# A forgetting attention and a gated convolution FFN on one core: the order of all 1,056 pieces of work written anew

## The chip, the core and the metric

The kernel runs on one core of a Trainium2 chip. The time is the device time of one launch in microseconds (us): the median of three runs was 245.37 us before the change (244.91 to 245.58). Everything said of the inside of a run comes from one profiled execution of the kernel before.

## What is computed

For each of 8 batches: an attention over 8 heads (576 tokens, 64 wide) whose scores carry a decay, then a feed-forward layer whose gate is a convolution of width 3 along the tokens.

```python
# attention, per batch and head: q, k, v [576, 64], f [576]
scores = q @ k.T / 8
cum    = cumsum(log(clip(f, 1e-4, 1)))
scores = where(j > i, -1e9, scores + cum[i] - cum[j])
attn   = softmax(scores) @ v                       # -> x [576, 512] over 8 heads
# feed-forward, per batch
h    = maximum(x @ w_in, 0)                        # [576, 1024]
conv = sum_k conv_w[k] * shift(h, k - 1)           # along the tokens
out  = (h * sigmoid(conv)) @ w_out                 # [576, 512], float32
```

## The kernel before

The work is cut into small named pieces, and a string `ORDER` lists them all in the order in which they are written into the program. Each engine (TensorE is PE in the profile, VectorE DVE, ScalarE ACT, GpSimd POOL, SyncE SP with its DMA queue) gets its own pieces in that order and works through them in order, so `ORDER` fixes what stands behind what on every engine and on every DMA queue. A piece that may run on several engines carries the engine behind an `@`. `ORDER` also decides which buffer a piece gets: there are four PSUM buffers (`ps0` to `ps3` in the rows below), and a piece that needs one takes the buffer that was given back longest ago in the list.

```python
for x in order:
    name, _, engine = x.partition("@")
    ...
    for r in t["take"]:
        self.slot[name, r] = free[r].pop(0)
```

The pieces, by the letters in `ORDER` (the head group `hb`, 0 to 15, is half of a batch, four heads; `i` is a pair of heads, 0 to 31; `b` is a batch; `ff` is one of eight slices of 128 hidden channels):

- Loading q and k. For `hb` 0 and 1: `ld` (DMA), nine transposes on TensorE (`tp`, L166), copied out of PSUM by ScalarE or VectorE (`cl`, L172 or L174). From `hb` 2 on: a transposing DMA (`q`, L180), for `hb` 2 to 7 followed by a clean-up on VectorE (`cl`, L186) and by two small DMAs of decay rows (`rw`, L204 and L205) from a table in HBM (`image`). That table is made once: the chain `dca`, `dcl` (the logarithm, L268 on ScalarE, then a table load), `dcs`, `dck` ends in the tile `kc`, and `ki` stores it with three DMAs (L281).
- v: DMAs `v`, casts to fp16 `va` (L219, and L221 for the last 64 tokens).
- Weights: DMAs `wi`, `wo` (L518), casts `wic`, `woc` (L526).
- Scores on TensorE: `sd` (diagonal blocks), `so` (the rest), `st` (the last 64 tokens), all L314. Their exponentials on ScalarE: `ed` (L355), `eo` (L372), `et` (L334). From `hb` 8 on the causal mask is laid on by GpSimd selects `md` and `mt` (L358, L337).
- `pv` on TensorE (attention times v, L391 and L396), `n` and `m` on VectorE (divide by the row sums, L405 and L407), `t` on TensorE and `tx` on VectorE or ScalarE (turn the result, L416 and L419; a DMA for `hb` 11 to 15).
- Feed-forward of batch `b`: `f` (L431) on TensorE, `r` (relu, L442) on ScalarE, `c` and `d` (the convolution: two VectorE operations that read two tensors each, L448 and L450), `a` (the gate's curve, L453) on ScalarE, `g` (gate times h, L460 or L458) on VectorE, `o` (L476) on TensorE, `e` (copy out, L481, L492) on ScalarE or VectorE, `s` (store).

The first feed-forward product `f0.0` needs both head groups of batch 0 turned (`tx0`, `tx1`), and `f1.0` those of batch 1 (`tx2`, `tx3`). After every `f` come `r`, `c`, `d`, `a`, `g` on two engines, and all eight `g` of a batch before its `o`. The list is a mix of the attention of later head groups and the feed-forward of earlier batches.

## Time and profile before

| what | value |
|---|---|
| median of the runs shown | 245.37 us (244.91 to 245.58) |
| the profiled execution: its span, first to last instruction | 244.7 us |
| TensorE busy | 228.6 us (93%) |
| ScalarE busy | 206.8 us (85%) |
| VectorE busy | 205.5 us (84%) |
| GpSimd busy | 51.9 us (21%) |
| first product of the feed-forward (`f0.0`) | at 37.30 us |
| first product of batch 1's feed-forward (`f1.0`) | at 63.23 us |
| last matmul ends | at 240.7 us |

The profiled execution has no device time of its own beside its span; the median of the runs lies 0.67 us above the span, and that part is taken as it is. Times inside the run are counted from the first instruction. "Busy" joins overlapping instructions of an engine; an engine that shows two instructions with x2 started the second before the first had ended.

### The profile page before, as it was taken

The page shows a single profiled execution, that of the slowest core. Times are in us where ns is not written, and L with a number is a line of the kernel's source. Part 1 is how long each engine was busy: PE and PEld are TensorE (multiplying, and loading weights), DVE is VectorE, ACT ScalarE, POOL GpSimd, SP SyncE. Part 2 cuts the span into 40 slices and gives each one's busy share as a digit, 9 for nine tenths or more (in the row PEclk, how much of TensorE's full clock was granted, in tenths as well). Part 3 has the DMA queues.
Part 4 walks back from the last instruction along what each step waited for, and adds up shares of the span by engine and source line. Part 5 has one row for each costly group of instructions (what it writes and reads, how often), then busy time and mean ns, then how long its engine had stood idle before and what let it go on. Part 6 is the DMA issues. An engine that isn't in the chain of part 4 may idle for free.

```text
span 244.7 us, 6393 instructions
## 1 busy us (share of the span) xinstructions
PE 228.6 (93%) x2627; PEld 146.1 (60%) x2627; DVE 205.5 (84%) x324; ACT 206.8 (85%) x278; POOL 51.9 (21%) x77
## 2 busy tenths in 40 slices
PE   0899889879999999999999999999999999999993
...
GB/s 189 334 169 250 278 184 189 223 198 306 196 216 196 169 182 220 238 268 251 224 212 274 194 198 269 270 102 196 265 198 227 195 209 4 106 173 77 171 85 216
DMA packets 120424, 49.68 MB, mean 203 GB/s; under 512 B 109879, under 2 KB 110647, under 8 KB 120395
## 3 DMA queue, kind: packets, MB, share of 16 engines
...
q10 hardware_dynamic: 322, 0.47, 0.6%
...
HBM read 21.11 MB, written 10.17 MB: 128 GB/s over the span
## 4 chain that ended last, share of the span: by engine, by line
PE 81%; DMA 5%; DVE 5%; ACT 5%; issue 1%; SPq 1%; ACTq 0%; DVEq 0%
PE ps L476 26%; PE ps L431 23%; PE ps L314 15%; PE ps L391 7%; DMA qk<-image 3%; PE ps L322 3%; PE ps L396 3%; DMA u<-in_f_dram 2%; PE ps L416 2%; ACT qk L172 2%; DVE u L450 2%; DVE u L448 1%; ACT ht L442 1%; ACT pp L372 1%; PE ps L317 1%
## 5 line engine op out<-in xcount | busy, mean ns | idle before, releaser
L431 PE MATMUL ps<-xt,w_in_f 128*128 128x512 f16 (+1 forms) x512 | 71.0, 288 | 0.4 <-DVE xt L419 0.4
L372 ACT ACTIVATE pp<-ps 128x1024 f16<-128x1024 f32 x64 | 64.8, 1032 | 3.7 <-PE ps L314 2.3
L476 PE MATMUL ps<-w_out_f,hg 128*128 128x512 f16 x288 | 66.8, 379 | 0.0
L314 PE MATMUL ps<-qk 128*128 128x128 bf16 (+2 forms) x576 | 63.9, 241 | 2.1 <-DMA qk<-image 0.9
L448 DVE SCALAR_TENSOR_TENSOR u<-ht,cwt 128x576 f32<-128x576 f16 x64 | 52.4, 832 | 4.4 <-ACT ht L442 4.2
L450 DVE SCALAR_TENSOR_TENSOR u<-ht,cwt,u 128x576 f32<-128x576 f16 x64 | 53.9, 856 | 0.5
L453 ACT ACTIVATE hg<-u,cw 128x576 f16<-128x576 f32 x64 | 48.7, 782 | 6.1 <-DVE u L450 6.0
L431 PEld LDWEIGHTS <-w_in_f 128*128 128x128 f16 x512 | 34.7, 99 | 29.4 <-issue 1.3
L314 PEld LDWEIGHTS <-qk 128*128 128x128 bf16 x576 | 39.4, 98 | 19.2 <-issue 2.5
L442 ACT ACTIVATE ht<-ps 128x576 f16<-128x576 f32 x64 | 41.0, 664 | 6.4 <-PE ps L431 2.8
L476 PEld LDWEIGHTS <-hg 128*128 128x128 f16 x288 | 26.9, 98 | 28.9
L460 DVE SCALAR_TENSOR_TENSOR hg<-hg,ht 128x576 f16<-128x576 f16 x51 | 38.6, 767 | 0.6 <-ACT hg L453 0.5
L358 POOL TENSOR_SCALAR_AFFINE_SELECT pp<-pd 128x1024 f16<-128x1024 f32 x16 | 19.7, 1244 | 53.6 <-ACT pd L355 53.6
L391 PE MATMUL ps<-va,pp 128*128 128x65 f16 x640 | 25.3, 194 | 1.7 <-DVE va L219 1.7
L391 PEld LDWEIGHTS <-pp 128*128 128x128 f16 x640 | 23.0, 98 | 4.2 <-DVE va L219 1.9
L407 DVE TENSOR_TENSOR xm<-ps,rc 128x896 f16<-128x896 f32 (+1 forms) x32 | 23.9, 751 | 0.5
L355 ACT ACTIVATE pp<-ps 128x1024 f16<-128x1024 f32 x16 | 16.6, 1038 | 5.2 <-PE ps L314 4.0
L219 POOL CAST va<-vf 128x1024 f16<-128x1024 f32 x8 | 10.0, 1247 | 34.3 <-PE ps L314 18.8
L355 ACT ACTIVATE pd<-ps 128x1024 f32<-128x1024 f32 x16 | 16.2, 1023 | 1.2 <-PE ps L314 0.5
L405 DVE RECIPROCAL rc<-ps 128x14 f32<-128x14 f32 (+1 forms) x32 | 6.6, 207 | 10.2 <-PE ps L396 4.9
L322 PE MATMUL ps<-mask,ident 128*128 128x512 bf16 (+1 forms) x40 | 14.4, 364 | 0.4 <-ACT pp L372 0.3
L481 ACT COPY ob<-ps 128x1024 f32<-128x1024 f32 (+1 forms) x14 | 12.9, 918 | 0.3 <-issue 0.2
...
## 6 DMA issues: line engine op xcount, KB each, us to landing
...
```

What stands on the lines that cost most here:

```text
L314: nc.tensor.matmul(o, tk[:, h * S + k0:h * S + k0 + 128], tq[:, h * S + q0:h * S + q0 + n], start=first, stop=last and not by_matmul(hb, h))
L355: nc.scalar.activation(o, ps_of(f"sd{i}").rearrange("p (s c) -> p s c", s=2), AF.Exp, scale=SCALE)
L372: nc.scalar.activation(pair(i)[:, s, 512:1536], ps_of(f"so{i}.{s}"), AF.Exp, scale=SCALE)
L391: nc.tensor.matmul(ps[:, c:c + D + 1], block(hb, h, m, n), va[:, h, m, 0:D + 1], start=(m == 0), stop=(m == n))
L407: nc.vector.tensor_tensor(xm[:, CUT * D * u:CUT * D * u + nj * k * D].rearrange("p (j x d) -> p j x d", x=k, d=D), got[:, :, :, 0:D], r.un ...
L431: nc.tensor.matmul(ps[:, t0:t1], w_in_f16[:, cc, 128 * ff:128 * (ff + 1)], xt[:, cc // 2, x:x + t1 - t0], start=(cc == 0), stop=(cc == NCC ...
L442: nc.scalar.activation(ht_of(b, ff)[:, 2:2 + S], ps_of(f"f{b}.{ff}")[:, 0:S], AF.Relu, scale=1.0 if (b, ff) in LATE else 0.5)
L448: nc.vector.scalar_tensor_tensor(u, ht[:, 1:1 + S], cwt[:, ff, 0:1], ht[:, 2:2 + S], op0=ALU.mult, op1=ALU.add)
L450: nc.vector.scalar_tensor_tensor(u, ht[:, 3:3 + S], cwt[:, ff, 1:2], u, op0=ALU.mult, op1=ALU.add)
L453: nc.scalar.activation(hg_of(b, ff), u_t[slot[f"c{b}.{ff}", "u"]], AF.Sigmoid if (b, ff) in LATE else AF.Tanh, scale=cw[:, ff, 1:2])
L460: nc.vector.scalar_tensor_tensor(hv, hv, 1.0, ht_of(b, ff)[:, 2:2 + S], op0=ALU.add, op1=ALU.mult)
L476: nc.tensor.matmul(ps[:, 512 * j:512 * (j + 1)], w, w_out_f16[:, ff, :], start=(ff == 0), stop=(ff == NFF - 1))
```

## The change

`ORDER` is replaced as a whole; no function and no instruction's shape is touched. The same 1,056 pieces stand in another order, and 38 of them name another engine:

- From GpSimd to VectorE: `va0.0`, `va0.1`, `va1.0`, `va6.0`, `va14.1`, `wic1`, `woc0`, `woc2`, `woc3`. From GpSimd to ScalarE: `va5.0`, `va9.1`, `va10.0`. To GpSimd: `va3.1`, `va7.1`, `va8.0`, `va12.1` from ScalarE, `va4.1`, `va7.0`, `va8.1`, `va9.0` from VectorE. GpSimd keeps its selects.
- From VectorE to ScalarE: `va1.1`, `cl1.1.0`, `tx0`, `e4.0`, `e7.3`, `e7.0`. From ScalarE to VectorE: `cl1.1.1`, `tx2`, `tx10`, `va11.1`, `e2.1`, `e7.1.0`, `e7.2`, `e7.4`.
- DMAs: `ki`, `rw1` and `s7.4` go from SyncE's queue to ScalarE's, `rw5` from ScalarE's to SyncE's.

The first two lines of the new list and of the old one:

```diff
-dca cw ld0 ld1 ld0.0.0 tp0.0.0 dcl ld0.1.0 ld0.0.1 tp0.0.1 tp0.1.0 v0.0 ld0.1.1 ld1.0.1 ld1.0.0 dcs dck v0.1 v0.2 ...
+ld0 ld0.0.0 dca tp0.0.0 ld0.0.1 tp0.0.1 cl0.0.0@ACT ld1 ld0.1.1 cl0.0.1@ACT v0.0 ld1.0.0 dcl cw ld0.1.0 tp1.0.0
+cl1.0.0@ACT v0.4 tp0.1.0 tp0.1.1 ld1.0.1 dcs cl0.1.0@ACT dck q2.0 cwt ki@ACT sd0 tp1.0.1 q2.1 tp1.1.0 cl0.1.1@DVE
```

The new `ORDER` has more lines, so a line of the changed kernel is 51 higher than the same line before (L172 is L223 there).

ScalarE at the start of the program. The row on `u0` is the logarithm `dcl`; rows with `qk` from `ps` are the copies `cl` of the turned q and k (`qk0` belongs to `hb` 0, `qk1` to `hb` 1); rows with `pp` are exponentials. Before:

```order
L268 ACTIVATE u0_120<-u0_120 128x576 [waits DMAHW2_49,DMAHW0_49,DVE_49]
L269 ACT_TABLE_LOAD
L172 ACTIVATE qk0_85<-ps1_130,lim_76 128x1152 [waits PE_49]
L172 ACTIVATE qk0_85<-ps2_131,lim_76 128x1152 [waits PE_49]
L172 ACTIVATE qk0_85<-ps3_132,lim_76 128x1152 [waits PE_49]
L355 ACTIVATE pp0_95<-ps2_131 128x2x512 [waits PE_49]
```

After:

```order
L223 ACTIVATE qk0_85<-ps0_129,lim_76 128x1152 [waits DVE_49,PE_49]
L223 ACTIVATE qk0_85<-ps1_130,lim_76 128x1152 [waits DVE_49,PE_49]
L319 ACTIVATE u0_120<-u0_120 128x576 [waits DMAHW2_49,DMAHW0_49,DVE_49]
L320 ACT_TABLE_LOAD
L223 ACTIVATE qk1_86<-ps3_132,lim_76 128x1152 [waits PE_49]
L223 ACTIVATE qk0_85<-ps0_129,lim_76 128x1152 [waits PE_49]
L332 DMA image_65<-kc_73 64x576 [waits DMAHW7_49,DVE_49]
L332 DMA image_65<-kc_73 64x576 [waits DMAHW0_49]
L332 DMA image_65<-kc_73 64x576 [waits DMAHW2_49,DVE_49]
L406 ACTIVATE pp0_95<-ps3_132 128x2x512 [waits PE_49]
```

Two copies now stand ahead of the logarithm, a copy for `hb` 1 (out of `ps3`, which the first exponential's scores take next) ahead of the third, and the three stores of the decay table stand in ScalarE's queue.

VectorE from the first value casts to the second turned tile, without the head of the list (`xt0` is batch 0's turned attention: the last row before is `tx1`, with `tx0` three rows above it). Before:

```order
L186 TENSOR_SCALAR qk2_87<-qk2_87,lim_76 128x2304 [waits DMAHW1_49]
L405 RECIPROCAL rc0_110<-ps1_130 128x14 [waits PE_49,Activation_49]
L407 TENSOR_TENSOR xm0_108<-ps1_130,rc0_110 128x896 [waits DVE_49]
L405 RECIPROCAL rc1_111<-ps1_130 128x4 [waits PE_49]
L407 TENSOR_TENSOR xm0_108<-ps1_130,rc1_111 128x256 [waits DVE_49]
L405 RECIPROCAL rc2_112<-ps3_132 128x14 [waits PE_49,Activation_49]
L407 TENSOR_TENSOR xm1_109<-ps3_132,rc2_112 128x896 [waits DVE_49]
L419 COPY xt0_113<-ps1_130 128x1152 [waits PE_49]
L405 RECIPROCAL rc0_110<-ps0_129 128x4 [waits PE_49,Activation_49]
L407 TENSOR_TENSOR xm1_109<-ps0_129,rc0_110 128x256 [waits DVE_49]
L419 COPY xt0_113<-ps3_132 128x1152 [waits PE_49]
```

After:

```order
L270 CAST va0_91<-vf0_89 128x4x4x64 [waits DMAHW6_49,DMAHW5_49,DMAHW1_49]
L270 CAST va1_92<-vf0_89 128x4x4x64
L272 CAST va1_92<-vf0_89 64x4x64
L237 TENSOR_SCALAR qk2_87<-qk2_87,lim_76 128x2304 [waits DMAHW4_49]
L456 RECIPROCAL rc0_110<-ps0_129 128x14 [waits PE_49,Activation_49]
L458 TENSOR_TENSOR xm0_108<-ps0_129,rc0_110 128x896 [waits DVE_49]
L577 CAST w_in_f16_69<-ob0_125 128x2x512 [waits DMAHW3_49]
L456 RECIPROCAL rc1_111<-ps2_131 128x4 [waits PE_49,Activation_49]
L458 TENSOR_TENSOR xm0_108<-ps2_131,rc1_111 128x256 [waits DVE_49]
```

(then `n1`, `m1` of `hb` 1 and one copy, `tx1`). Three value casts and a weight cast came in, and the copy `tx0` went to ScalarE.

VectorE around `tx3`, the copy into `xt1` that lets `f1.0` start (`u` rows are `c` and `d`, `hg` rows are `g`). Before:

```order
L186 TENSOR_SCALAR qk1_86<-qk1_86,lim_76 128x2304
L419 COPY xt1_114<-ps3_132 128x1152
L450 SCALAR_TENSOR_TENSOR u2_122<-ht4_119,cwt_72,u2_122 128x576
L460 SCALAR_TENSOR_TENSOR hg_124<-hg_124,ht3_118 128x576
L460 SCALAR_TENSOR_TENSOR hg_124<-hg_124,ht2_117 128x576
L460 SCALAR_TENSOR_TENSOR hg_124<-hg_124,ht0_115 128x576
L460 SCALAR_TENSOR_TENSOR hg_124<-hg_124,ht1_116 128x576
L460 SCALAR_TENSOR_TENSOR hg_124<-hg_124,ht4_119 128x576
L448 SCALAR_TENSOR_TENSOR u1_121<-ht3_118,cwt_72 128x576
```

After:

```order
L470 COPY xt1_114<-ps1_130 128x1152
L237 TENSOR_SCALAR qk1_86<-qk1_86,lim_76 128x2304
L499 SCALAR_TENSOR_TENSOR u2_122<-ht4_119,cwt_72 128x576
L511 SCALAR_TENSOR_TENSOR hg_124<-hg_124,ht3_118 128x576
L501 SCALAR_TENSOR_TENSOR u2_122<-ht4_119,cwt_72,u2_122 128x576
L511 SCALAR_TENSOR_TENSOR hg_124<-hg_124,ht0_115 128x576
L511 SCALAR_TENSOR_TENSOR hg_124<-hg_124,ht2_117 128x576
L511 SCALAR_TENSOR_TENSOR hg_124<-hg_124,ht1_116 128x576
L511 SCALAR_TENSOR_TENSOR hg_124<-hg_124,ht4_119 128x576
L577 CAST w_out_f16_70<-ob1_126 128x1024
L577 CAST w_out_f16_70<-ob0_125 128x1024
L499 SCALAR_TENSOR_TENSOR u3_123<-ht3_118,cwt_72 128x576
```

The clean-up `cl5.1` and the convolution half `c0.7` moved from ahead of the copy to behind it, and weight casts (`woc3`, `woc0`, a few rows later `woc2`) now stand on VectorE.

More of the change, by code (lines that the diff above doesn't have):

```diff
@@ new lines @@
+ld0 ld0.0.0 dca tp0.0.0 ld0.0.1 tp0.0.1 cl0.0.0@ACT ld1 ld0.1.1 cl0.0.1@ACT v0.0 ld1.0.0 dcl cw ld0.1.0 tp1.0.0
+cl1.0.0@ACT v0.4 tp0.1.0 tp0.1.1 ld1.0.1 dcs cl0.1.0@ACT dck q2.0 cwt ki@ACT sd0 tp1.0.1 q2.1 tp1.1.0 cl0.1.1@DVE
+cl1.0.1@DVE sd1 v0.3 tp1.1.1 ed0 v0.2 cl1.1.0@ACT ed1 so1.1 v0.1 so0.1 so1.0 wi1 cl1.1.1@DVE cl2.0 va1.0@DVE st0 wi0
+rw1@ACT eo0.1 wic0@POOL va0.0@DVE so0.0 eo1.0 eo1.1 wi2 sd2 wic2@POOL va0.1@DVE cl2.1 rw2@SP et0 eo0.0 so2.1 ed2 pv0.0
+eo2.1 so2.0 sd3 n0.0 m0.0 so3.0 eo2.0 q3.0 st1 wic1@DVE q3.1 ed3 pv0.1 et1 so3.1 eo3.0 eo3.1 sd5 va1.1@ACT ed5 pv1.0
@@ new lines @@
+pv1.1 n0.1 m0.1 t0 n1.0 m1.0 n1.1 m1.1 so5.1 tx0@ACT t1 sd4 eo5.1 ed4 wi3 tx1@DVE f0.0 cl3.1 q4.1 r0.0 so4.1 cl3.0
+f0.1 f0.2 eo4.1 r0.1 v1.0 v1.3 c0.0 so4.0 d0.0 f0.3 wic3@POOL rw3@SP so5.0 r0.2 eo4.0 h0 q4.0 f0.4 c0.1 v1.2 r0.3 v1.1
+eo5.0 f0.5 a0.0 r0.4 wo3 c0.2 st2 et2 v1.4 d0.2 cl4.1 d0.1 g0.0 a0.2 st3 sd6 c0.3 r0.5 c0.4 ed6 so6.1 g0.2 eo6.1 d0.4
+d0.3 q5.0 sd7 va2.0@DVE f0.6 so7.1 ed7 eo7.1 va3.0@ACT c0.5 va3.1@POOL pv2.0 et3 q5.1 va2.1@POOL cl4.0 so6.0 n2.0 d0.5
+r0.6 a0.4 m2.0 rw4@ACT g0.4 wo1 so7.0 f0.7 c0.6 pv2.1 n2.1 eo6.0 eo7.0 r0.7 d0.6 pv3.0 pv3.1 a0.5 m2.1 v2.0 sd9 cl5.0
@@ new lines @@
+t2 n3.0 n3.1 v2.1 a0.3 m3.0 v2.2 a0.1 m3.1 ed9 so9.1 a0.6 tx2@DVE t3 st4 et4 sd8 tx3@DVE eo9.1 f1.0 cl5.1 woc1@POOL
+ed8 so9.0 eo9.0 c0.7 g0.3 r1.0 wo0 d0.7 so8.1 g0.5 g0.6 f1.1 eo8.1 f1.2 f1.3 a0.7 f1.4 r1.2 v2.4 rw5@SP g0.1 g0.7 r1.1
+v2.3 r1.3 woc3@DVE sd10 r1.4 wo2 woc0@DVE q6.0 ed10 c1.0 c1.2 so10.1 st5 et5 sd11 q6.1 woc2@DVE c1.1 c1.3 d1.2 q7.0
+d1.3 q7.1 so11.1 f1.5 eo10.1 o0.0 va5.0@ACT ed11 d1.1 d1.0 o0.1 o0.2 va4.0@ACT eo11.1 va5.1@ACT h1 v3.0 f1.6 cl6.0
+a1.2 c1.4 cl6.1 a1.1 e0.0@ACT rw6@SP g1.1 va4.1@POOL g1.2 a1.3 v3.2 v3.1 so10.0 a1.0 o0.3 r1.5 so8.0 r1.6 f1.7 cl7.0
@@ new lines @@
+eo10.0 v3.3 eo8.0 e0.1@ACT g1.3 c1.5 so11.0 pv4.0 d1.4 d1.5 pv4.1 cl7.1 eo11.0 r1.7 n4.0 m4.0 zc pv5.0 n4.1 a1.4 n5.0
+sd13 m4.1 pv5.1 m5.0 so13.1 a1.5 va7.0@POOL n5.1 ed13 sd12 rw7@SP c1.7 m5.1 c1.6 eo13.1 t4 so13.0 t5 ed12 tx4@DVE
+so12.0 eo13.0 sd15 tx5@DVE g1.4 eo12.0 va6.0@DVE q9.1 f2.0 d1.7 ed15 so12.1 g1.0 r2.0 eo12.1 f2.1 d1.6 st7 q9.0 a1.7
+c2.0 et7 so15.1 pv6.0 g1.7 a1.6 r2.1 f2.2 v4.0 v3.4 f2.3 eo15.1 q8.1 n6.0 st6 m6.0 sd14 g1.6 c2.1 r2.3 d2.0 et6 g1.5
+r2.2 ed14 so15.0 c2.2 h2 q8.0 c2.3 f2.4 d2.2 so14.1 f2.5 eo15.0 a2.0 r2.5 o1.0 a2.2 so14.0 eo14.1 d2.3 g2.0 va7.1@POOL
@@ new lines @@
+fi9 r2.4 c2.5 o1.1 d2.5 eo14.0 a2.5 e1.0@ACT c2.4 f2.6 fi8 g2.2 pv7.0 va6.1@POOL sd18 pv7.1 d2.1 v4.4 r2.6 n7.0 pv6.1
+m7.0 ed18 n7.1 g2.5 a2.1 n6.1 m7.1 m6.1 sd16 ed16 so16.0 eo16.0 g2.1 v4.2 t7 t6 tx6@DVE f2.7 v5.0 v4.1 tx7@DVE sd19
+f3.0 o1.2 a2.3 d2.4 r2.7 q10.1 st9 md18 c2.7 r3.0 md16 ed19 v4.3 c2.6 d2.6 q11.0 so18.0 a2.4 va8.0@POOL c3.0 a2.6 g2.6
+et9 eo18.0 g2.3 md19 va8.1@POOL s1.0 sd17 ed17 q11.1 o1.3 q10.0 f3.1 so19.1 so19.0 md17 d2.7 g2.4 d3.0 e1.1@ACT r3.1
+f3.2 f3.3 mt9 eo19.1 va9.0@POOL so17.0 eo19.0 s0.0 o1.4 a2.7 eo17.0 h3 r3.2 r3.3 a3.0 g2.7 fi11 f3.4 c3.1 d3.1 so18.1
```

28 lines of the change are left out of this document (27 added, 1 removed).

## The prediction

> **What bounds the kernel now.** I read the page first: the busy shares, the slices and the chain of waits.
>
> ```profile
> span 244.7 us, 6393 instructions
> PE 228.6 (93%) x2627; PEld 146.1 (60%) x2627; DVE 205.5 (84%) x324; ACT 206.8 (85%) x278; POOL 51.9 (21%) x77
> PE   0899889879999999999999999999999999999993
> PE 81%; DMA 5%; DVE 5%; ACT 5%; issue 1%; SPq 1%; ACTq 0%; DVEq 0%
> ```
>
> TensorE is most of the chain, and its slices have holes in the first quarter only. Next, the busy time by stretch (length, then PE, PEld, DVE, ACT, POOL busy, granted clock, DMA share, GB/s):
>
> ```profile
> 10.00:20.00 10.00, 9.92 (x120) 8.29 (x119) 5.19 (x12) 7.74 (x8) 1.37 (x2) 1.00 1.01 221
> 20.00:30.00 10.00, 9.23 (x122) 6.89 (x120) 4.48 (x5) 7.89 (x10) 3.06 (x3) 1.00 1.05 270
> 37.30:63.20 25.90, 22.75 (x293) 15.14 (x290) 24.30 (x36) 22.55 (x33) 4.59 (x4) 0.93 1.10 226
> 63.20:88.10 24.90, 24.90 (x288) 15.32 (x286) 23.32 (x33) 23.62 (x33) 3.17 (x2) 1.00 0.98 197
> 88.10:240.70 152.60, 152.56 (x1659) 92.24 (x1659) 139.37 (x211) 136.06 (x189) 32.27 (x33) 1.00 0.86 193
> ...
> 38.20:63.10 24.90, 22.00 (x283) 14.71 (x283) 23.51 (x36) 21.73 (x32) 4.59 (x4) 0.93 1.09 234
> 63.10:86.70 23.60, 23.60 (x255) 14.25 (x254) 22.02 (x32) 22.63 (x32) 3.17 (x2) 1.00 0.98 194
> ```
>
> From 63 us to 240.7 TensorE has no gap (24.90 of 24.90, 152.56 of 152.60). So the end of the program is the moment at which TensorE reaches a given piece, plus the matmuls that are left. The pieces ahead of `f0.0`, between `f0.0` and `f1.0`, and between `f1.0` and `sd12` (where 88.08 stands below) are the same sets in both lists, only shuffled; so the time of `sd12` decides, if TensorE stays without gaps behind it. Between `f0.0` and `f1.0` TensorE works 22.75 of 25.90 us, part of it at half clock (mean 0.93, worth 1.8 us): about 20.9 us of matmul at full clock in 25.9. Who holds it up there? The waits of TensorE between 37 and 63 us (who waits, for whom: total, times, longest):
>
> ```profile
> PE ps L391 <- DVE va L219: 1.7, 1, 1.7
> PE ps L314 <- DVE xm L407: 0.5, 1, 0.5
> PE ps L431 <- DVE xt L419: 0.4, 1, 0.4
> PE ps L416 <- DVE xm L407: 0.3, 1, 0.3
> ```
>
> VectorE, four times in a row, and it is busy 23.51 of 24.90 us there. It is the bound from 38 to 63 us, and close to it up to 87 (22.02 of 23.60).
>
> **The change, part by part.** The rows for the prices (start, busy, engine, line; in brackets the idle time ahead and its releaser), first the head of the program:
>
> ```profile
> 9.65 3.71 ACT L172 ACTIVATE qk<-ps,lim 128x1152 uint16<-128x1152 uint16 x3
> 10.26 0.76 DVE L276 SCALAR_TENSOR_TENSOR kc<-u,kc 64x576 bf16<-64x576 f32 x1
> 12.22 0.58 PE L322 MATMUL ps<-mask,ident 128*128 128x512 bf16 x1
> 23.25 1.43 SPq L518 DMA_DIRECT2D ob<-in_moe_w_in_dram  x3
> 25.15 7.33 DMA qk<-image
> 32.52 0.40 PE L314 MATMUL ps<-qk 128*128 128x128 bf16 x4 [0.86 <-DMA qk<-image]
> 35.75 0.75 DVE L419 COPY xt<-ps 128x1152 f16<-128x1152 f16 x1
> 37.51 0.76 DVE L419 COPY xt<-ps 128x1152 f16<-128x1152 f16 x1 [0.46 <-PE ps L416]
> ```
>
> 1. *The head, up to `tx1`* (ends 37.51 + 0.76 = 38.27). Two copies (3.71 / 3 = 1.24 each) now run ahead of the logarithm, which takes nothing from it; but the first scores `sd0` take the buffer that the copy `cl1.0.0` empties behind the logarithm. They start at 12.22 now. Ends: 1.2 earlier (`kc` is ready at 10.26 + 0.76 = 11.02, and nothing else is in the way), or one copy, 1.2, later. I take 1.0 later, since that copy waits for the fifth load of the queue and stands behind the table load. ScalarE, which must empty every score buffer, idles 2.26 and 2.11 us of the two slices from 10 to 30; it gives one copy to VectorE and takes one, so this delay is made up by about 25 us. The gain comes behind it. Now the decay rows of `hb` 2 are issued behind three weight loads (23.25 x3) and land 7.33 us later, and `sd5` waits for them until 32.52. In the new list the weight loads stand directly behind the value loads, several microseconds ahead of the rows, and `sd5` is reached at about 30.4 without that wait. What follows is ScalarE's exponentials, so only some 1.3 of these 2.1 us reach `pv1.0`. The copy `tx0` (0.75, of which 0.67 to the next start) leaves VectorE, where `n1.1`, `m1.1` and `tx1` stood behind it. The four casts that VectorE gets there (0.6 each) lie in its idle time: it works 4.48 of 10 us from 20 to 30. Sum: -1.3 - 0.67 = -2.0, `tx1` ends at 36.3. Ends: -3 (all of `sd5`'s 2.1 counts) and +1 (the delay of `sd0` stays).
>
> The rows for VectorE behind it:
>
> ```profile
> 38.18 1.75 DVE L186 TENSOR_SCALAR qk<-qk,lim 128x2304 uint16<-128x2304 uint16 x2
> 49.25 0.68 DVE L219 CAST va<-vf 128x1024 f16<-128x1024 f32 x1
> 57.34 1.48 DVE L450 SCALAR_TENSOR_TENSOR u<-ht,cwt,u 128x576 f32<-128x576 f16 x1
> 61.42 1.03 DVE L186 TENSOR_SCALAR qk<-qk,lim 128x2304 uint16<-128x2304 uint16 x1
> 62.38 0.74 DVE L419 COPY xt<-ps 128x1152 f16<-128x1152 f16 x1
> 68.61 1.00 DVE L448 SCALAR_TENSOR_TENSOR u<-ht,cwt 128x576 f32<-128x576 f16 x1 [0.51 <-ACT ht L442]
> 69.53 2.31 DVE L450 SCALAR_TENSOR_TENSOR u<-ht,cwt,u 128x576 f32<-128x576 f16 x2
> 73.34 1.54 DVE L448 SCALAR_TENSOR_TENSOR u<-ht,cwt 128x576 f32<-128x576 f16 x2
> 85.61 1.09 DVE L407 TENSOR_TENSOR xm<-ps,rc 128x896 f16<-128x896 f32 x1
> 86.62 0.17 DVE L405 RECIPROCAL rc<-ps 128x4 f32<-128x4 f32 x1
> 123.34 1.58 DVE L219 CAST va<-vf 128x1024 f16<-128x1024 f32 x1
> ```
>
> An undisturbed `c` or `d` lasts 0.81, and the next starts 0.73 after it (1.54 for two). Beside a GpSimd cast or select they stretch: 1.48 at 57.34, 2.31 instead of 1.54 at 69.53, 1.00 at 68.61. That is what "kept apart" can save.
>
> 2. *VectorE from `tx1` to `tx3`*: now 62.38 + 0.74 - 38.27 = 24.85 us. Out go `c0.7` (0.73), `cl5.1` (0.96, to the next start) and the stretched part of `d0.6` (1.48 - 0.81 = 0.67), in comes `tx2` (0.67): 24.85 - 1.69 = 23.2. `tx3` ends at 59.5, `f1.0` starts there; now it starts right behind 63.12. TensorE's own 20.9 us fit into 23.2.
>
> 3. *VectorE from `tx3` to `m5.0`* (now 85.61 + 1.09 - 63.12 = 23.6). In come `c0.7` 0.73, `cl5.1` 0.88 (1.75 / 2), three weight casts at 0.6 (0.68 less the overlap with the next), 1.8, and `n4.1`, `m4.1`, 0.5; out go `va4.1`, 0.2, and the stretched parts 0.19 + 0.77. Sum +2.75: 26.3, so `m5.0` ends at 85.8. Before the change TensorE had `so13.1` waiting for it, then `pv5.1` and `sd12`; now `sd12` itself takes the buffer. TensorE alone would be there at 59.5 + 24.9 = 84.4, so VectorE decides: `sd12` at 85.8.
>
> ```profile
> 88.08 0.38 PE L322 MATMUL ps<-mask,ident 128*128 128x512 bf16 x1
> ```
>
> 85.8 against 88.08: **-2.3 us**.
>
> 4. *Everything behind `sd12`.* The other engine changes and all other selects kept apart lie here, where TensorE has no gap that they could fill: 0. The cover is thinner for VectorE, which gets some 1 us more, and stays ample: it works 139.37 of 152.60 now. ScalarE gets nine pieces of arithmetic and gives twelve away. The last copy is one of 512 columns on ScalarE with one store, instead of two halves on two engines and queues: some 0.2 us either way, taken as 0.
>
> 5. *DMA issues on ScalarE's queue* (`ki`, `rw1`). In the trace such an issue does not stop the arithmetic:
>
> ```profile
> 52.83 1.04 ACT L372 ACTIVATE pp<-ps 128x1024 f16<-128x1024 f32 x1
> 52.97 0.66 ACTq L205 DMA_DIRECT2D qk<-image  x1
> 53.73 0.41 ACT L221 CAST va<-vf 64x256 f16<-64x256 f32 x1
> ```
>
> But `rw1` waits for `cl1.1.1`, now on VectorE, and the exponential `eo0.1` stands behind it: about 1 us of ScalarE's idle time, in the 26.1 at which I let the last `eo` of `hb` 0 end.
>
> The sum is made against the profiled span of 244.7; the median is 0.67 above it, and I carry that over: 245.37 - 2.3 = 243.1 us.
>
> **The rivals.**
>
> *B, a larger gain.* VectorE's idle time in the two stretches (24.90 - 23.51 = 1.4, 23.60 - 22.02 = 1.6) goes too, because more ready work stands in its queue. With all of it gone `sd12` stands at 82.8, still behind TensorE's own 36.4 + 20.9 + 24.9 = 82.2: -5.3. Half of it is likelier: -3.8, 241.6. For it: these waits are on ScalarE's relu and on matmuls, which come earlier too. Against: the work is in a fixed order, and the new list has as many links.
>
> *C, no difference.* The casts now on VectorE are stretched in their turn: the cast at 123.34 took 1.58 beside a select, that at 49.25 took 0.68, so a hit costs 0.9. Ahead of `sd12` GpSimd keeps seven or eight casts of thirteen. With two hits `sd12` stands at 87.6, -0.5: 244.9. The Trainium skill (SBUF — State Buffer, section Who interferes with whom) speaks for this rival: a VectorE cast in a two-port mode and a GpSimd instruction take one shared port pair as an exclusive lock, and the second to come waits. The rows at 57.34 and 123.34 agree with it. By that rule moving a cast to VectorE does not take it out of the conflict, it only changes who is hit.
>
> *D, slower.* The decay rows of `hb` 1 (`rw1`), now on ScalarE's queue while weights and transposing loads fill the other, land as late as those of `hb` 2 did: 7.33 us after an issue at about 20.7, so at 28.0 instead of the 24.9 at which `sd2` is reached. TensorE and ScalarE both stand, +3.1 on the head: -2.3 + 3.1 = +0.8, 246.2 us. It decides from a landing later than about 27.2. Against: before the change TensorE waits for such rows once only, the 0.86 us at 32.52.
>
> That the change does not keep the two engines apart would be C.
>
> **How the numbers follow.** A difference under 0.3% (0.74 us) can hardly be told from none here. The forecast (-0.8 to -3) gets 0.49, B (beyond -3) 0.16, C 0.16, D with any other late head 0.19. Faster 0.65, same 0.16, slower 0.19. The lower end, 241.2, lies a little beyond the likelier value of B; the upper end, 245.9, takes in C and the nearer half of D; beyond both lie some 2 in 10.
>
> **What would show it.** Right: TensorE without gaps from about 60 us on; `tx1` ending near 36.3, `tx3` near 59.5, `sd12` near 85.8; no `c` or `d` over 1.1 us ahead of `sd12`; the mean granted clock between `f0.0` and `f1.0` nearer to 1 than 0.93. Wrong: a TensorE gap behind 90 us longer than 0.5 us, which would mean that VectorE or ScalarE ran out of cover (point 4); `sd2` later than 27 (D); VectorE casts of 1.3 us and more ahead of `sd12` (C); `f0.0` later than 37.3, which would undo term 1.

## The result: slower, 252.16 us instead of 243.1

The changed kernel takes 252.16 us (median of four runs, 251.25 to 253.28), the one before, run beside it, 245.48 us. The ratio is 1.0246, 95% interval 1.0208 to 1.0284: 6.0 us slower. Ratios leave out runs that took over 1.5% more than the fastest of the same kernel; medians don't. The profiled execution has a span of 250.5 us against 244.7, 5.8 more. Its page, the lines that answer to those shown of before (span, busy shares, TensorE's slices, the chain that ended last):

```profile
span 250.5 us, 6396 instructions
PE 228.8 (91%) x2627; PEld 146.4 (58%) x2627; DVE 214.4 (86%) x331; ACT 206.0 (82%) x275; POOL 47.2 (19%) x73
PE   1699999879999999989999999999998699999990
PE 67%; DVE 10%; DMA 10%; SPq 5%; ACT 3%; issue 2%; DVEq 0%; ACTq 0%
```

TensorE's work is the same. Its share of the chain fell from 81% to 67%, and transfers with their queue (DMA and SPq) rose from 6% to 15%. The slices show holes near 108 us (the 8 in the middle) and near 193 (the 8 and the 6), where before there were none. The stretches from `f0.0` to `f1.0`, `f1.0` to `sd12`, and `f2.0` to the last matmul (length; PE, PEld, DVE, ACT, POOL busy; clock, DMA share, GB/s):

```profile
61.42:86.09 24.67, 24.67 (x286) 15.14 (x284) 24.54 (x38) 24.23 (x33) 0.68 (x2) 1.00 1.04 214
89.94:244.05 154.11, 149.32 (x1616) 89.63 (x1613) 143.26 (x208) 130.90 (x182) 34.09 (x34) 1.00 0.87 188
37.45:61.42 23.97, 20.95 (x293) 14.23 (x290) 22.65 (x35) 22.01 (x32) 3.46 (x4) 1.00 1.09 219
```

The last of these stretches before the change:

```profile
91.81:240.67 148.86, 148.86 (x1614) 89.40 (x1613) 135.84 (x204) 132.56 (x185) 30.89 (x31) 1.00 0.85 194
```

The 5.8 us come out of three pieces. `f2.0` starts 1.87 us earlier (89.94, 91.81). From there to the last matmul the new kernel needs 5.25 us more (154.11, 148.86), of which 4.79 are time without a matmul (154.11 - 149.32). Behind the last matmul it needs 2.4 more (250.5 - 244.05 against 244.7 - 240.67). So between these two profiles the head brought nearly what was forecast, and all behind it lost 7.7 us that were forecast as 0.

The head's part doesn't hold up against other profiles of the same two lists. Two kernels of the experiments below, `b_nosel` and `head_old`, follow the old list unchanged past `f1.0`. Their stretches from `f0.0` to `f1.0`, in this order:

```profile
36.74:61.94 25.20, 21.47 (x293) 14.40 (x291) 23.96 (x36) 22.82 (x33) 4.65 (x4) 1.00 1.15 230
```

```profile
36.52:61.50 24.98, 21.31 (x292) 14.43 (x290) 23.67 (x36) 22.59 (x33) 3.66 (x4) 1.00 1.05 223
```

TensorE had its full clock there (1.00, where the kernel before shows 0.93), `f1.0` came at 61.94 and 61.50 instead of 63.23, and `sd12` at 86.74 and 86.89 instead of 88.08. Of the five profiles with the new list and its loads up to `sd12` (`head_new` has two further pieces directly ahead of it), the changed kernel's 86.09 is the earliest: `a_vhigh` has 86.10, `a_nosel` 86.34, `head_new` 87.73, `end_old` 88.88. The means are 87.24 (old, three profiles) and 87.03 (new, five). So a gain of 2 us at `sd12` is not shown: it comes from a late profile of the old list beside an early one of the new.

TensorE's waits in the new kernel (who, for whom: total, times, longest):

```profile
PE ps L482 <- DMA xt<-xm: 1.9, 1, 1.9
PE ps L442 <- DVE va L270: 1.7, 1, 1.7
PE ps L365 <- DVE xm L458: 1.7, 4, 0.7
...
PE ps L365 <- DMA qk<-image: 0.8, 1, 0.8
PE ps L365 <- DMA qk<-blank: 0.6, 1, 0.6
```

Three kinds: transfers (the turned result of `hb` 13, and the decay images of `hb` 9 and 8), a cast that itself waits for a load, and VectorE's normalization. The wait for the cast, at 50 us, was as long before the change (1.7 us). The places, in rows of the timeline (start, busy, what; in brackets the idle time ahead):

```profile
36.77 0.76 DVE L470 COPY xt<-ps 128x1152 f16<-128x1152 f16 x1 [0.38 <-PE ps L467]
60.52 0.76 DVE L470 COPY xt<-ps 128x1152 f16<-128x1152 f16 x1 [0.19 <-PE ps L467]
84.42 1.36 DVE L458 TENSOR_TENSOR xm<-ps,rc 128x256 f16<-128x256 f32 x2
86.09 0.38 PE L373 MATMUL ps<-mask,ident 128*128 128x512 bf16 x1
106.56 0.61 PE L365 MATMUL ps<-qk 128*128 128x128 bf16 x8 [0.64 <-DMA qk<-blank]
109.46 1.06 PE L365 MATMUL ps<-qk 128*128 128x128 bf16 x12 [0.81 <-DMA qk<-image]
192.09 0.61 PE L365 MATMUL ps<-qk 128*128 128x128 bf16 x8 [0.72 <-DVE xm L458]
199.96 0.65 PE L482 MATMUL ps<-xt,w_in_f 128*128 128x512 f16 x4 [1.89 <-DMA xt<-xm]
```

What stands ahead of the images in SyncE's queue:

```profile
92.55 1.33 SPq L262 DMA_DIRECT2D vf<-in_v_dram  x2
93.93 2.86 SPq L231 DMA_TRANSPOSE qk<-in_k_dram  x1
96.84 3.60 SPq L231 DMA_TRANSPOSE qk<-in_q_dram  x1
100.56 1.51 SPq L246 DMA_DIRECT2D qk<-blank  x2
102.12 0.64 SPq L248 DMA_DIRECT2D qk<-image  x1
102.87 1.42 SPq L246 DMA_DIRECT2D qk<-blank  x2
104.33 0.63 SPq L248 DMA_DIRECT2D qk<-image  x1
```

Each row begins where the one before it ended. Adding up the issue rows between 36 and 116 us gives 76.2 of 80 us in the new kernel and 77.0 in the old: this queue was nearly full in both, and I had not read it.

The longest wait, 1.89 us, has another history. SyncE's rows ahead of it:

```profile
184.46 2.94 SPq L262 DMA_DIRECT2D vf<-in_v_dram  x3
192.10 1.35 SPq L473 DMA_TRANSPOSE xt<-xm  x1
193.49 0.72 SPq L262 DMA_DIRECT2D vf<-in_v_dram  x1
194.32 1.49 SPq L473 DMA_TRANSPOSE xt<-xm  x1
```

Here the queue stood idle from 187.4 us until VectorE's normalization had ended (192.03). The input of the second turning was ready at 193.17, but a load of v stood ahead of it, and TensorE went on at 199.96. VectorE and the queue made this wait together.

### The profile page after: what moved, and what is told of

Same layout as the page of the kernel before. It is cut to its first block, busy times and chain, and to the rows that moved or that the text cites. A ratio compares the mean times of both kernels' runs of the same rounds, so it can differ in the third digit from the quotient of the medians.

```text
span 250.5 us, 6396 instructions
## 1 busy us (share of the span) xinstructions
PE 228.8 (91%) x2627; PEld 146.4 (58%) x2627; DVE 214.4 (86%) x331; ACT 206.0 (82%) x275; POOL 47.2 (19%) x73
## 3 DMA queue, kind: packets, MB, share of 16 engines
q1 hardware_dynamic: 119833, 48.59, 90.1%
## 4 chain that ended last, share of the span: by engine, by line
PE 67%; DVE 10%; DMA 10%; SPq 5%; ACT 3%; issue 2%; DVEq 0%; ACTq 0%
PE ps L527 21%; PE ps L482 19%; PE ps L365 13%; PE ps L442 4%; DVE xm L458 3%; SPq L231 3%; DVE u L501 3%; DMA hg<-in_q_dram 3%; DVE u L499 2%; PE ps L373 2%; DMA xt<-xm 2%; PE ps L467 2%; DMA qk<-image 2%; DMA u<-in_f_dram 2%; DMA vf<-in_v_dram 2%
## 5 line engine op out<-in xcount | busy, mean ns | idle before, releaser
L482 PE MATMUL ps<-xt,w_in_f 128*128 128x512 f16 (+1 forms) x512 | 69.7, 286 | 1.9 <-DMA xt<-xm 1.9
L365 PE MATMUL ps<-qk 128*128 128x128 bf16 (+2 forms) x576 | 64.6, 241 | 3.2 <-DVE xm L458 1.7
L501 DVE SCALAR_TENSOR_TENSOR u<-ht,cwt,u 128x576 f32<-128x576 f16 x64 | 56.6, 898 | 0.4
L499 DVE SCALAR_TENSOR_TENSOR u<-ht,cwt 128x576 f32<-128x576 f16 x64 | 54.4, 865 | 0.7 <-ACT ht L493 0.5
L511 DVE SCALAR_TENSOR_TENSOR hg<-hg,ht 128x576 f16<-128x576 f16 x51 | 40.2, 802 | 1.4 <-ACT hg L504 1.2
L442 PE MATMUL ps<-va,pp 128*128 128x65 f16 x640 | 24.5, 193 | 2.3 <-DVE va L270 1.7
L442 PEld LDWEIGHTS <-pp 128*128 128x128 f16 x640 | 22.4, 97 | 4.3 <-DVE va L270 2.0
L217 PE MATMUL ps<-ident_b,hg 128*128 128x128 bf16 x72 | 7.4, 276 | 7.4 <-DMA hg<-in_q_dram 6.4
L270 POOL CAST va<-vf 128x1024 f16<-128x1024 f32 x6 | 8.2, 1377 | 26.3 <-DVE xm L458 20.6
```

The source lines that it names most:

```text
L365: nc.tensor.matmul(o, tk[:, h * S + k0:h * S + k0 + 128], tq[:, h * S + q0:h * S + q0 + n], start=first, stop=last and not by_matmul(hb, h))
L442: nc.tensor.matmul(ps[:, c:c + D + 1], block(hb, h, m, n), va[:, h, m, 0:D + 1], start=(m == 0), stop=(m == n))
L482: nc.tensor.matmul(ps[:, t0:t1], w_in_f16[:, cc, 128 * ff:128 * (ff + 1)], xt[:, cc // 2, x:x + t1 - t0], start=(cc == 0), stop=(cc == NCC ...
L499: nc.vector.scalar_tensor_tensor(u, ht[:, 1:1 + S], cwt[:, ff, 0:1], ht[:, 2:2 + S], op0=ALU.mult, op1=ALU.add)
L501: nc.vector.scalar_tensor_tensor(u, ht[:, 3:3 + S], cwt[:, ff, 1:2], u, op0=ALU.mult, op1=ALU.add)
L511: nc.vector.scalar_tensor_tensor(hv, hv, 1.0, ht_of(b, ff)[:, 2:2 + S], op0=ALU.add, op1=ALU.mult)
```

## The experiments

Every kernel has the same pieces; most are a list put together from the two. Ratios are to the kernel before, 5 rounds each.

| kernel | ratio, 95% interval |
|---|---|
| the changed kernel | 1.0246 (1.0208 to 1.0284) |
| `head_new` / `head_old` | 1.0036 (1.0000 to 1.0071) / 1.0217 (1.0149 to 1.0285) |
| `f1_new` | 1.0113 (1.0073 to 1.0153) |
| `end_old` | 1.0193 (1.0140 to 1.0246) |
| `engines_new` | 1.0941 (1.0874 to 1.1007) |
| `sp_old` / `casts_back` | 1.0248 (1.0204 to 1.0293) / 1.0225 (1.0162 to 1.0288) |
| `a_nosel` / `b_nosel` | 1.0180 (1.0125 to 1.0235) / 1.0010 (0.9981 to 1.0039) |
| `a_vrow` / `b_vrow` | 0.9986 (0.9950 to 1.0023) / 0.9991 (0.9953 to 1.0030) |
| `a_v5` | 1.0073 (1.0033 to 1.0113) |
| `a_vlow` / `a_vhigh` | 1.0086 (1.0053 to 1.0119) / 1.0111 (1.0074 to 1.0147) |
| `a_all` | 0.9937 (0.9900 to 0.9975) |
| `q_old` / `q_new` | 1.0478 (1.0436 to 1.0521) / 1.0350 (1.0304 to 1.0395) |
| `q_old_end` | 1.0446 (1.0409 to 1.0482) |

**Which stretch: `head_new` and `head_old`, cut at `sd12`.**

```diff
 head_new: the new list up to sd12, then the old one's rest
-sd12 rw7@SP c1.7 m5.1 c1.6 eo13.1 t4 so13.0 t5 ed12 ...
+v3.4 g1.0 sd12 va6.0@POOL c1.7 t4 d1.7 eo13.1 m5.1 ed12 rw7@SP ...
 head_old: the old list up to sd12, then the new one's rest
-sd12 va6.0@POOL c1.7 n5.1 m4.1 t4 d1.7 ...
+m4.1 va7.0@POOL n5.1 sd12 rw7@SP c1.7 m5.1 c1.6 eo13.1 t4 ...
```

> The new list up to `sd12`, then all remaining pieces in the order (and on the engines) of the old list. In the profiles the new list has `sd12` 2.0 us earlier (86.09 against 88.08). If that gain is real and the old rest holds it, 245.5 - 2.0 = 243.5 us. Rival: the rest has a floor of its own (the queue that loads the images, VectorE), which lies close under the old times, so that the gain is eaten behind `sd12`: 245.5 us, with new gaps of TensorE behind 100 us.

> The old list up to `sd12`, then all remaining pieces as in the new list. Between `sd12` and the end the new list loses 5.3 us on TensorE and 2.4 us behind its last matmul. If all of it belongs to the rest alone, the program takes 252.2 + 2.0 = 254.2 us. Rival: part of the loss comes from TensorE being early; then the 1.7 us at 104 to 110 (waits for the images of `hb` 9 and 8) vanish, and it takes 252.2 to 252.5.

The loss sits in the rest: with the new rest alone 2.2% remain (250.8 us on the scale of 245.5, under both figures expected, with a wide interval). `head_new` is no faster than before, so the new head alone gains nothing. In its profile (an execution of 249.3 us, above its median of 247.49) `f1.0` is at 60.90, even earlier than in the changed kernel, but `sd12` at 87.73, and VectorE says why. Two of its rows, a weight cast and a clean-up of loaded q:

```profile
70.88 0.70 DVE L526 CAST w_out_f<-ob 128x1024 f16<-128x1024 f32 x1 [0.95 <-DMA ob<-in_moe_w_out_dram]
...
80.33 0.88 DVE L186 TENSOR_SCALAR qk<-qk,lim 128x2304 uint16<-128x2304 uint16 x1 [0.74 <-DMA qk<-in_q_dram]
```

VectorE waits for loads at places where the profile of the changed kernel shows no wait. The list is the same up to there. `end_old`, with the same list, shows such waits too (1.1 and 1.0 us), and `a_nosel` shows none: what differs between executions is when the loads landed.

**An earlier cut: `f1_new`, at `f1.0`.**

```diff
 new list up to f1.0, then the old one's rest
-f1.0 cl5.1 woc1@POOL ed8 so9.0 ...
+wo0 v2.3 v2.4 c0.7 woc3@POOL woc1@POOL cl5.1 rw5@ACT woc0@POOL ed8 f1.0 so9.0 ...
```

> The new list up to `f1.0`, the remaining pieces as in the old list. Three profiles of the new head have `f1.0` at 60.9 to 62.2 us against 63.23; what they lose again they lose between 70 and 92 us, where VectorE waits for a weight load (`woc2`, 0.95 and 1.15 us) and for the load behind `cl7.0` (0.74 and 1.00 us). If those waits take the gain, the old order behind `f1.0`, which has neither cast on VectorE, keeps it: 245.5 - 1.8 = 243.7 us. Rival: the loads themselves set the pace (one queue, in order), and any early head is stopped by them: 245.5 us.

Missed by 5 us: 1.1% slower. Taking the waits for `woc2` and `cl7.0` away did not keep the gain. Its profile is its fastest run (`f1.0` at 60.98, the last matmul at 240.73, the old value), so where the median loses more was not seen. It does show where the earlier `f1.0` was lost. TensorE waited 1.17 and 0.32 us for ScalarE's exponentials behind `f1.0`, and `sd12` came at 87.73. No load is named among these waits:

```profile
64.71 0.60 PE L314 MATMUL ps<-qk 128*128 128x64 bf16 x4 [1.17 <-ACT pp L355]
```

**The end: `end_old`.**

```diff
 new list up to o7.4.0, then the old one's rest, which ends with
-... o7.0.6 e7.2@DVE o7.0.7 s7.2@SP e7.0@ACT s7.0@SP
+... e7.0@DVE s7.0@SP o7.1.0 ... o7.1.7 e7.1.0@ACT e7.1.1@DVE s7.1.0@ACT s7.1.1@SP
```

> The new list up to `o7.4.0`, then the remaining pieces in the order of the old list: the last output chunk is again the one that is split in halves over two engines and two queues. Behind the last matmul the new kernel needs 6.4 us, the old one 4.06. If the order of the last chunks and their stores makes that, 252.2 - 2.4 = 249.8 us. Rival: the late last pieces of the gate (`g7.6`, `g7.7`) set the end in either order, then 252 us, with a gap of TensorE ahead of the last matmuls.

Behind the last matmul its profile needs 4.30 us. Over all profiles, ten kernels with the new end need 5.4 to 6.4 us there (mean 5.9), nine with the old end 4.0 to 4.7 (mean 4.2): 1.7 us. (`engines_new`, whose old end runs on other engines, needs 5.0.) The changed kernel's last issues, after a matmul that ended at 244.05:

```profile
244.12 0.54 SPq L558 DMA_DIRECT2D out_dram<-ob  x1
244.71 0.58 SPq L559 DMA_DIRECT2D out_dram<-ob  x1
245.40 0.53 SPq L549 DMA_DIRECT2D out_dram<-ob  x1
246.04 0.37 SPq L549 DMA_DIRECT2D out_dram<-u  x1
```

The last three copies end within 1.1 us of one another, their stores queue one behind the other, and the last one is 256 KB and leaves 1.3 us after its copy (244.15 + 0.59). The first two rows are `s7.4`. The new list names ScalarE's queue for it, but the kernel doesn't follow the list there:

```python
def store_chunk(name, b, c, n0, n1, e):
    if c == 4:
        return store(name, b, c)
    ...
```

`store` always uses SyncE's queue, so `s7.4` did not change its queue with the list. Its copy had ended at 242.62, and its two stores hold the queue for 1.2 us ahead of the last two. What the end would gain with `s7.4` on the other queue was not tried. The total improved by 0.5% only, less than expected, with overlapping intervals.

**Engines without the order: `engines_new`.**

```diff
 old list, order unchanged, 38 pieces on the new list's engines, e.g.
-wic1@POOL ... woc0@POOL ... va6.0@POOL ... ki@SP
+wic1@DVE ... woc0@DVE ... va6.0@DVE ... ki@ACT
```

> The old list with its order unchanged, but each of the 38 pieces on the engine or queue that the new list gives it. If the order alone is to blame, about 245.5 us, within 1. Rival: VectorE's additional casts and copies (some 3 us of work) are to blame, since it works 139.4 of 152.6 us behind `sd12` already: 248 us or more, with waits of TensorE for VectorE.

9.4% slower, by far the largest effect. VectorE's waits for transfers in it:

```profile
DVE va L219 <- DMA vf<-in_v_dram: 5.5, 1, 5.5
...
DVE w_in_f L526 <- DMA ob<-in_moe_w_in_dram: 4.6, 1, 4.6
```

The rival's time came true, but these are waits for loads and not a lack of time on VectorE. On GpSimd, which works a fifth of the span, a cast could wait for its load without harm; at the same place on VectorE all that stands behind it waits too. In the new order the changed kernel's VectorE waits only 0.33 us ahead of its first value casts. How much of the 9.4% the casts make was not separated: TensorE's own longest wait behind its start is one of 4.4 us for decay rows, and the DMAs `ki` and `rw1` of such rows change their queue in this kernel too.

**Queue order and casts: `sp_old`, `casts_back`.**

```diff
 sp_old, SyncE's queue
-v3.3 zc rw7 q9.1 q9.0 v4.0 v3.4 q8.1 h2 q8.0 fi9 fi8 v4.4
+v3.3 v3.4 zc rw7 q9.1 q9.0 q8.1 h2 q8.0 fi9 fi8 v4.0 v4.4
 casts_back, same order
-wic1@DVE woc0@DVE woc2@DVE woc3@DVE
+wic1@POOL woc0@POOL woc2@POOL woc3@POOL
```

> The new list with two loads moved on SyncE's queue: `v3.4` behind `v3.3`, as in the old list, and `v4.0` behind `fi8`, so that neither stands between the loads of q and k for `hb` 9 and 8. They take 1.33 us of the queue there. If the queue's order makes the two waits of TensorE at 106 and 109 us (0.64 and 0.81, 1.7 us of loss in all) and nothing behind them has slack of its own, 252.2 - 1.4 = 250.8 us. Rival: VectorE sets the end behind that, then 252.2 us, and the gaps at 133 to 139 or at 186 to 200 us grow by what is won.

> The new list with the four weight casts that it gives to VectorE (`wic1`, `woc0`, `woc2`, `woc3`) back on GpSimd, at the same places in the list. In profiles of the new head VectorE waited 0.95 and 1.15 us in its queue for the load of `woc2`. If such waits in VectorE's queue cost the new list time, 252.2 - 1 = 251.2 us, VectorE without a wait for the weights. Rival: on GpSimd they stretch the two-operand operations beside them, as the change wanted to avoid: 252.2 us or more, with `c` or `d` over 1.1 us between 60 and 75 us.

Neither moves the time measurably. In `sp_old` TensorE's idle time at 100 to 110 us went from 1.45 us to none, but 1.27 us appeared at 91 to 93, where the rows of `hb` 7 were now late: in this full queue, moving one load ahead made another late.

**GpSimd's selects: `a_nosel`, `b_nosel`.**

```diff
 def diag_exp(i):   (the tail likewise)
-    o = pair(i)[:, :, 0:512] if i // 2 in MASK_PE else pd_t[slot[f"ed{i}", "pd"]]
+    o = pair(i)[:, :, 0:512]
 def diag_mask(i):
-    nc.gpsimd.affine_select(...)
+    return
```

> The new list without GpSimd's selects: the masks of `hb` 8 to 15 are left out (the exponentials of those blocks are taken at scale 0, so that they stay finite, and are written straight to their place), all else is the same. In the new profile the two-operand operations of VectorE take 151.2 us in all instead of 141.9 at their undisturbed durations, 9.3 us too much (3.0 in the old one, and 0.9 in a cast); some 60% of the overlap is with selects. If these make VectorE late and so the gaps of TensorE at 133 to 139, 186 to 192 and 197 to 200 us, 252.2 - 4.2 = 248.0 us. Rival: the gaps are waits along a chain of links that has no slack in this order, whatever the duration of one operation: 251.7 us or more.

> The old list without GpSimd's selects, in the same way. TensorE has no gap behind 63 us there, so both theories say 245.5 us, within 0.7. It is the measure for the same edit in the new list: less than 244.8 would mean that leaving the selects out helps by another way than VectorE's waits.

Both leave out the causal masks of `hb` 8 to 15; the exponentials concerned are taken at scale 0, so that they stay finite. The old list doesn't care. The new one gains some 1.6 us, but the intervals overlap, and not the 4.2 us of the theory. In its profile (252.46 us, its median is 251.76) TensorE's waits for VectorE's normalization fell from 1.7 us in four to 0.9 in one, and its idle time at 130 to 140 us from 0.53 us to none. Its waits for the cast of v and for `blank` grew, from 1.7 to 2.4 and from 0.6 to 1.7. So contention was a part at most.

**The loads: `a_vrow`, `b_vrow`.**

```diff
 def load_v(b, kb):
-    n = 128 if kb < NKB - 1 else SL
-    nc.sync.dma_start(vf[0:n, :, kb, :], ... ap=[[D, n], [S * D, H], [1, D]])
+    if kb == NKB - 1:
+        return
+    nc.sync.dma_start(flat[:, 640 * kb:640 * (kb + 1)], ... ap=[[512, 128], [1, 640]])
```

> The new list, with v loaded as rows: each of four DMAs for a batch moves 2560 contiguous bytes per partition (wrong elements of v, 11% more bytes, a tenth of the packets; the fifth DMA is left out). In the new profile the DMA engines' share is 1.07 to 1.22 in nearly every 10 us from 30 to 160 us. If the loads' pace makes TensorE's losses at 49 to 51 (1.9, a cast that waits for v), at 104 to 110 (1.7) and the spread from run to run, 252.2 - 3.6 = 248.6 us or less. Rival: VectorE and the links of the list set the end; then 251.5 us or more.

> The old list with the same edit. Its losses that come from loads are 1.84 us at 48 to 50 (the same cast) and 1.05 at 31 to 33 (decay rows). If the loads set the pace there too, 245.5 - 2.5 = 243 us, and the new list remains slower by what it loses elsewhere (its end and VectorE), 4 to 6 us. Rival: the old list is paced by VectorE and TensorE alone, 245.5 us.

Each of four DMAs for a batch now moves 2560 contiguous bytes per partition, which are the wrong elements of v, and the fifth, for the last 64 tokens, is left out. This shows the main cause. With light loads the new list is level with the old one, 6.4 us faster than with its own loads (0.9986 against 1.0246), and the old list gains nothing. The rival of the second expectation, that the old list isn't paced by loads, holds; my guess of 243 was wrong. The packets of the changed kernel, then of `a_vrow`:

```profile
DMA packets 120424, 49.68 MB, mean 198 GB/s; under 512 B 109879, under 2 KB 110647, under 8 KB 120395
q1 hardware_dynamic: 119833, 48.59, 90.1%
```

```profile
DMA packets 87527, 50.72 MB, mean 208 GB/s; under 512 B 72887, under 2 KB 73655, under 8 KB 87499
q1 hardware_dynamic: 86937, 49.64, 83.5%
```

More bytes, fewer packets, less time on the transfer engines. SyncE's issue rows between 36 and 116 us fall from 76.2 to 66.0 us. The Trainium skill (DMA: Bandwidth & Descriptors, section Why small descriptors are slow) puts a fixed cost on every packet, 27% for one of 256 B; the share that fell from 90.1% to 83.5% of a shorter span agrees in direction. And the stretch from `f2.0` to the last matmul in `a_vrow`:

```profile
89.09:238.56 149.47, 148.56 (x1617) 89.34 (x1613) 141.69 (x208) 130.73 (x182) 33.84 (x32) 1.00 0.80 193
```

149.47 us instead of 154.11: 4.6 of the 5.25 us. Yet VectorE is as busy and as stretched there as before the edit. Its two-operand groups in that stretch, of the changed kernel and of `a_vrow` (busy, mean ns):

```profile
L501 DVE SCALAR_TENSOR_TENSOR u<-ht,cwt,u 128x576 f32<-128x576 f16 x50 | 45.7, 923 | 0.2
L499 DVE SCALAR_TENSOR_TENSOR u<-ht,cwt 128x576 f32<-128x576 f16 x48 | 41.1, 870 | 0.4 <-ACT ht L493 0.2
```

```profile
L452 DVE SCALAR_TENSOR_TENSOR u<-ht,cwt,u 128x576 f32<-128x576 f16 x50 | 44.6, 901 | 0.2
L450 DVE SCALAR_TENSOR_TENSOR u<-ht,cwt 128x576 f32<-128x576 f16 x48 | 41.9, 887 | 0.4 <-ACT ht L444 0.2
```

And of the kernel before:

```profile
L450 DVE SCALAR_TENSOR_TENSOR u<-ht,cwt,u 128x576 f32<-128x576 f16 x49 | 40.5, 840 | 0.4
L448 DVE SCALAR_TENSOR_TENSOR u<-ht,cwt 128x576 f32<-128x576 f16 x49 | 40.3, 837 | 3.0 <-ACT ht L442 2.8
```

So the new list did not keep the engines apart on the chip (923 and 870 ns against 840 and 837), but with the loads in time that cost nothing measurable (0.9986).

**Packets or issues; which half: `a_v5`, `a_vlow`, `a_vhigh`.**

```diff
 a_v5: rows of v, but five DMAs for a batch (the fifth takes the last 64 columns)
 a_vlow: light loads if b < 4; a_vhigh: if b >= 4
```

> The new list with v loaded as rows once more (wrong elements of v), but in five DMAs for a batch as in the original, so that the number of issues and the eight DMAs that may be under way at a time are as before, and only the packets are fewer and longer. If the packets on the DMA engines make the loads slow, the time stays at that of the four-DMA version, 246.2 us within 1. Rival: the issues in SyncE's queue make it, each waiting for the landing of the eighth before it; then a good part of the gain is lost, 249 us or more.

> The new list with v loaded as rows (four DMAs of 2560 contiguous bytes per partition, wrong elements) for batches 0 to 3 alone, whose loads lie ahead of 86 us. In the new profile the loss by loads ahead of 90 us is the 1.9 us at 49 to 51 and what differs from run to run. If the loss behind `sd12` is one of its own, 252.2 - 2 = 250.2 us. Rival: loads that lag early make all later ones late through the one queue; then the early half gives most of the 6.0 us that light loads won in all: 248 us or less.

> The same for batches 4 to 7 alone, whose loads lie behind 92 us. If the losses at 104 to 110 (images behind loads of `v4` and of q and k) and at 197 to 200 us (a transposing DMA behind a load of `v7`) are made there, 252.2 - 3.7 = 248.5 us. Rival: the lag is made early; then it stays at 251 us or more.

`a_v5` takes 247.3 us on the scale of 245.5, between the two figures expected. Fewer packets win 1.73% of the 2.60%, and without the fifth issue it is 0.87% more (the intervals of `a_v5` and `a_vrow` don't meet). That the transfer engines and the queue are both limits is my reading; these runs don't part them fully, since an issue with few packets is shorter too (those of v between 36 and 116 us take 16.1 us for 21 in the changed kernel, 10.0 for 21 in `a_v5`, 6.9 for 15 in `a_vrow`). The early half alone comes to 247.6 us on the scale of 245.5, as the rival of `a_vlow` said, the late half to 248.2, as the expectation of `a_vhigh` said. Either half alone wins more than half of the whole (1.6% and 1.35%), so the loss is not made at one place. That loads are late throughout and any relief lets the rest catch up fits this, but is not shown link by link.

**All three: `a_all`.** New list, light loads, no selects, old end; it leaves out the masks and the right elements of v.

> The new list with the three edits together: v loaded as rows, no selects (masks of `hb` 8 to 15 left out), the end in the old order. If loads, selects and the last stores make all of the loss, their sum is 3.6 + 1.6 (measured for the selects) + 2.1 (the end, by the profile of `end_old`): 252.2 - 7.3 = 244.9 us. Rival: the order itself, with its tight links between engines, keeps 3 us or more: 248 us or more.

0.9937, 244.0 us on the scale of 245.5, 0.9 under the sum of the three parts. `f2.0` is 1.94 us earlier than in the kernel before, and 0.87 earlier than in `b_vrow` (90.74), the old list with light loads; in `a_vrow` it is 1.65 earlier (89.09). So with light loads the new head does gain. The stretch behind it takes 148.62 us, 0.24 less than in the kernel before:

```profile
89.87:238.49 148.62, 148.60 (x1616) 89.21 (x1613) 133.80 (x206) 130.94 (x183) 8.27 (x8) 1.00 0.78 196
```

**Loads and arithmetic crossed: `q_old`, `q_new`, `q_old_end`.**

```diff
 q_old: the new list's arithmetic, all loads in the old list's order and places
-sd7 va2.0@DVE f0.6 so7.1 ed7 ... pv2.0 et3 q5.1 ...
+sd7 va2.0@DVE f0.6 q5.0 so7.1 q5.1 ed7 ... pv2.0 et3 ...
 q_new: the reverse; q_old_end: q_old with the old end
```

> The new list with all its loads (q, k, v, weights, decay rows, images) in the order, on the queues and at the places of the old list: each stands behind as many TensorE pieces as in the old one, 18 a little earlier where a piece needs it; all arithmetic, the transposing DMAs of the results and the stores as in the new list. With light loads of v the new list lost nothing (246.2). If the new order of the loads is what it loses by, 252.2 - 4 = 248 us or less. Rival: any order of these loads is too slow for the new order of the arithmetic, whose pieces ask for them earlier: 251 us or more.

> The reverse: the arithmetic of the old list with the loads of the new one. If the new order of the loads is bad by itself, 245.5 + 3 = 248.5 us or more, with waits of TensorE or VectorE for loads that the old list does not have. Rival: it does no harm where nothing else has been moved, 246.5 us or less.

> The loads of the old list as in the first of these runs, and the end from `o7.4.0` on in the old order. By the profile of `end_old` the old end saves 2.1 us behind the last matmul: 2 us less than the run with the old loads alone, 246 us if that gives 248. Rival: the last pieces of the gate are late anyway; then no more than 1 us less.

Both crossings are worse than either list (4.8% and 3.5%). `q_new` came out as expected (248.5 us or more). My expectation of 248 us for `q_old` missed by ten: the new order of the loads is not bad, it fits the new arithmetic better than the old one does. What each list has is a fit of the two; the old end saves 0.3% here, within the intervals, as the rival of `q_old_end` said. No kernel of this study that does the whole computation beats the one before.

## Why the prediction was wrong, point by point

*Term 1, the head to `tx1`: mechanism partly right, size off.* `tx1` ended at 36.77 + 0.76 = 37.53 instead of 36.3, a gain of 0.74 and not 2.0. The delay of `sd0` was there (13.68), but was not made up by 25 us: `sd2` started at 26.81, `sd5`, without its wait as foreseen, at 32.33 instead of 30.4.

*Terms 2 and 3: right in sum by luck, twice.* `tx1` to `tx3` took 61.28 - 37.53 = 23.75 us (forecast 23.2), `tx3` to the end of `m5.0` 85.78 - 61.28 = 24.50 (forecast 26.3). `sd12` came at 86.09 against a forecast 85.8: -1.99 instead of -2.3. The first luck is that the errors cancel. `f1.0` came 1.9 us later than forecast, and it was TensorE and not VectorE that set `sd12` from there: it worked 24.67 of 24.67 us and did not wait for `m5.0`. The second is the 88.08 from which I counted. The same old list had `sd12` at 86.74 and 86.89 in two other profiles, without the half clock that I had seen (0.93) and taken as covered by VectorE. Between `f1.0` and `sd12` GpSimd does next to nothing (0.68 of 24.67 us), and the clock stayed at 1.00. But a stretched `c` was there after all, 1.50 us at 39.39, beside a weight cast.

*Step 4, "Everything behind `sd12`: 0": this is the step that failed.* It measured +5.25 on TensorE and +2.4 behind it. I took a TensorE without gaps as a sign that everything behind it had slack, and looked for cover on VectorE and ScalarE alone. The DMA shares of 1.0 and more stood in my own quoted rows, and SyncE's queue was nearly full from 36 to 116 us; a list that asks for its loads in another order, or 2 us earlier, finds none of that slack. With light loads in both lists the loss was gone (0.9986 and 0.9991). The sign that I gave for failure appeared (gaps of 0.64, 0.81, 0.72 and 1.89 us behind 90 us), but I had put it down to VectorE or ScalarE in advance: two of the four are waits for loads, one is for VectorE, and the longest is for a transfer that VectorE and the queue had made late together. The end, "some 0.2 us either way", cost 1.7 to 2.4.

*Point 5, issues on ScalarE's queue:* not tested by itself; `sd2` stayed under 27, so rival D's mechanism did not decide.

*Rival C* had half of it: the conflict was moved, not removed. But not as I priced it: no large cast on VectorE was stretched (0.68 and 0.69), the two-operand operations were. *Rival D* had the right sign and the right resource (a load that lands late), at the wrong place: one landing in the head, instead of the whole queue behind it.

What stays open: why the fastest run of `f1_new` and its median differ by more than 1 us, how the loss by loads divides between packets and issues, and which pairs of pieces make the crossed lists so slow. The runs showed the resource, not each link.
